# Side matmul steps as row slices, 64-bit shifts on GpSimd, and residual slots by position, in an attention block with a parallel GELU layer

## The chip, the core and the metric

The kernel runs on one NeuronCore of a Trainium2 chip. The metric is device time in microseconds of one execution. The engines are TensorE (PE in the profile, its weight loads PEld), VectorE (DVE), ScalarE (ACT), GpSimd (POOL) and the queue that issues transfers (SP).

## What is computed

A transformer block with attention and a feed-forward layer side by side, both fed by one layer norm:

```python
# x: 2048 x 512 bf16; H = 32 heads of Dh = 16; one key and one value head for all (wk, wv: 512 x 16)
xn = layernorm(x)
q = (xn @ wq) as 32 heads; k = xn @ wk; v = xn @ wv
p = softmax(q k^T * Dh**-0.5)            # 32 x 2048 x 2048
a = (p @ v, heads joined) @ wo
h = gelu_tanh(xn @ w1 + b1)              # F = 1792
out = x + a + (h @ w2 + b2)
```

## The kernel before

**Tiles and units.** The 2048 query rows are taken in four blocks of 512 (`TBW`), the heads in groups of four, so there are 32 groups (three blocks of eight, and a last block cut by quarters of its queries). A group has 64 score tiles of 128 keys x 512 columns. Three tiles in a row make a unit; there are 683 units. A unit's scores (`scores`, line 987) are three matmuls of 32 contraction rows each, one per head. They lie in three of the four 32-row groups of the array side by side, and write three PSUM banks; two halves of three banks alternate between units, so the scores of unit u+2 wait until unit u's banks are read. Unit u leaves row group (3u+3) mod 4 empty.

**Two ways to the exponential.** `DTAB` says for each tile of each unit which engine makes it. A tile not named goes to ScalarE: one ACTIVATE (`exp`, line 1026) covers the unit's one, two or three such tiles. A named tile goes to VectorE (`p1`, line 1057): it writes a 16-bit integer that, read as bf16, is a piecewise-linear power of two, and four copies shifted by constants (`SPL_STEPS`) are summed with fitted weights by TensorE. So a ScalarE tile costs TensorE one product with V, and a VectorE tile five (`pv_mm`, line 1069). Tiles of VectorE are closed into batches of one to six (`close_batch`, line 1075). A batch has three steps: the first writes one shifted copy (tile 1 from 0, +26), the second two copies (+51), both on VectorE at line 1104; the third shifts tile 0 in place (-26), one instruction per tile, written for GpSimd at line 1100, which the planner may give to VectorE.

**Side work.** Between the scores TensorE also makes the projections: q (`q_pack`, line 1195), the hidden layer (`h_mm`, 1230), and the output tiles (`out_tile`, 1302: 14 steps of `w2`, four of `wo`, one of `b2`). Each step is a 128-row contraction cut into four matmuls of 32 output columns (`mm4`, line 686). They lie in the four column groups side by side and accumulate in PSUM bank 7 (`pM`). One job at a time holds that bank; VectorE reads it out. Products with V are column-group matmuls too. So TensorE changes between row mode (a score visit) and column mode all along.

**Order.** Nothing is scheduled at run time. `Prog.schedule` (line 241) simulates the five engines with a cost for each operation and fixes each engine's order; `emit` writes it with semaphore waits. TensorE's next operation is chosen by `pick_pe`. Operations of kind `pl` (the third steps, and the normalization of the attention output, lines 1139 and 1179) are put on GpSimd under a VectorE operation that doesn't use the port that the two share; operations marked `lock` do use it. Where VectorE would be free, it takes a `pl` operation itself. The tables `HP`, `YP`, `QK`, `Q3` say at which unit each side job is released. Where TensorE would stand still for long, the planner puts in filler matmuls on zeros (line 1430).

**Residual.** An output tile needs x again: `x_load` brings it into slot 14 or 15 of `x_sb` (tile number mod 2), `out_tile` adds PSUM to it there, and `store` sends it out.

Of the kernel before, what the change touches and what calls it, by code (L numbers as in the profile page):

```python
# [5 lines left out]
dt = mybir.dt  # L6
# [34 lines left out]
PL_OCC = 0.62  # L41
# [8 lines left out]
PL_FREE = 0.06  # L50
NE_ND_KB = (23, 19, 11, 6)
# [8 lines left out]
TBL = 1  # L60
QSP = 1
# [3 lines left out]
DTAB = "o0t02o.02to.0to2o0.o.t22o.002.o0.o220t.2o.22o000.o.002ot00.o202.o200.0202.t.2t2.2t2t.20o2o0t..0.00o.o0t0o2ot0..t22tt20o202o2.ot.t.t2t.t0toto.00to.2oot.2oo002t.0t.202o.oo.22t.2o22t20.axXXo2toto.tt0t2t2.2oo202.t0tt.t0t0.oo2000o.to.0ot0.2o2t02o22t22.t220t0.20.o02.0t.0to0t22.t0..020t2o2.2.t2o2.220o02..0o00o02t...22t0oo.20t20tt.02o0t202..o2o..022to2o..02ot.00o2tt.00o0o200oo2..2t2to02o..0t0o2t2o.0tt2.2t20o..2t0ttttoo.00ot.22o.t.to222o20t.22o020..oto.o0t200ot0.0oo0.o02..22o222t..02o02ot0.0t0.2tt2.0o0t0to.0tt0000Ba0XXaot022o02.o00..too2o2.tt2o.20to00ot..2o22o0oott0o.002.o2.2tt.2t0oo0t0.ot00o.tt20.ot0.0t2.oo.0t0tt2t.2tttt.00o0tot.t2t0.0o2oo..ot22o20t200ot..t00.0t.to02o2ot0.0to2.2.t.."  # L65
YF = 664
# [48 lines left out]
class _Op:  # L115
    __slots__ = ("eng", "fn", "deps", "sdeps", "stream", "amt", "need", "ticket", "waits", "clock", "occ", "lat",
                 "allow", "kind", "tag", "nun", "outs", "rel", "lock", "pm", "rdy", "start", "end", "vis", "idx", "done", "due", "real", "docc")


class Prog:  # L120
# [19 lines left out]
    def add(self, eng, fn, r=(), w=(), acc=None, dma=None, occ=0.1, lat=0.15, allow=1.0, kind=None, tag=None, after=(), due=None, lock=False, docc=0.0):  # L140
        op = _Op()
        op.lock, op.docc = lock, docc
# [10 lines left out]
        op.pm = any(k == ("bank", 7) or k[0] == ("bank", 7) for k in w)  # L153
# [21 lines left out]
        if acc is not None:  # L175
            dep(self.writer.get(acc), False)
            for o in self.readers.get(acc, ()):
                dep(o, False)
        op.deps = list(deps.values())
# [8 lines left out]
        if acc is not None:  # L188
            self.accs.setdefault(acc, []).append(op)
# [15 lines left out]
    def pick_pe(self, t, cand, allr, mode, visit, cgbusy):  # L205
        S = [o for o in cand if o.kind == "S"]
        rest = [o for o in cand if o.kind != "S"]
# [27 lines left out]
    def rank(self):  # L235
        s0 = next(o.idx for o in self.ops if o.kind == "S")
        due = iter(PRO_DUE)
        for op in self.ops[:s0]:
            op.due = (op.due or 0.0) if op.stream != op.eng else next(due)

    def schedule(self):
# [36 lines left out]
        s_seen = False  # L278
        vleft = sum(op.kind == "v" for op in ops)
# [3 lines left out]
        def seen(o):  # L283
            return max(o.rdy + (PL_TAKE if o.kind == "pl" else 0.0), lockend) if o.lock else o.rdy

        while left:
# [12 lines left out]
            cand = [o for o in able[e] if seen(o) <= t + 1e-9]  # L299
# [100 lines left out]
            if e == "pe":  # L400
# [25 lines left out]
                elif op.kind != "side":  # L426
                    m = {"S": "row", "side": "col"}.get(op.kind, "full")
                    w = 0.0 if m == mode else SW_ROW if m == "row" else SW_COL if m == "col" else SWITCH
                    st = max([t, pend + w] + [c + w for c in cgbusy])
                    op.start = st  # L430
                    op.end = st + op.occ * slow
                    op.vis = op.end + op.lat
                    area += op.occ * (0.75 if op.kind == "S" else 1.0)
                    recent.append((st, op.occ * (0.75 if op.kind == "S" else 1.0)))
                    if m == "col":
                        cgbusy = [op.end] * 4
                    mode = m
# [11 lines left out]
            if e == "act" and op.kind in ("exp", "gelu"):  # L449
                aend = max(op.end + A_LAG, aend + op.occ + A_INC)  # L450
                op.vis = aend + A_SEM
            free[e] = max(free[e], op.end)
# [5 lines left out]
            order.append(op)  # L458
            left -= 1
            for o, cross in op.outs:  # L460
                o.nun -= 1
                v = op.vis if cross else op.end
                if v > o.rdy:
                    o.rdy = v
                if o.nun == 0:
                    ready[o.eng].append(o)
# [4 lines left out]
        for op in order:  # L471
            if op.kind == "pv":
                g, cg, first = op.tag
                op.fn = (lambda e, f=op.fn, a=first, b=last[(g, cg)] is op: f(e, a, b))
        self.nfill = nfill
# [4 lines left out]
    def settle(self):  # L480
        free = {e: 0.0 for e, _ in self.SECTIONS}
        mode, cg, pend, aend, r1 = None, [0.0] * 4, 0.0, 0.0, 0.0
        for op in self.ops:
# [3 lines left out]
            if op.eng == "pe":  # L487
                if op.kind in ("pv", "side") or (op.kind == "fill" and occ > 0.15):
# [5 lines left out]
                    mode, end = "col", t + 0.006  # L494
                else:
                    m = "row" if op.kind == "S" else "full"
# [3 lines left out]
                pend = t + (min(occ, C_OCC) if mode == "col" else occ)  # L500
            else:
# [53 lines left out]
def bass_parallel_sum__grouped_kv_mqa__dense_activation_gelu__prompt_kernel(  # L555
# [33 lines left out]
    with ExitStack() as es:  # L589
# [76 lines left out]
        def B(b):  # L666
            return ("bank", b)
# [25 lines left out]
        M4 = [(("bank", 7), j) for j in range(4)]  # L693

# [258 lines left out]
        late = [pr.writer["ibi"]]  # L953
        dma("sp", wop[:], A_wo.rearrange("(g p) n -> p g n", p=P), "d_wo", w=["wop"], after=late)
# [3 lines left out]
        dma("sp", b2row[0:1, :], B_b2.rearrange("(o n) -> o n", o=1), "d_b2", w=["b2row"])  # L958

# [27 lines left out]
        def scores(u):  # L987
# [17 lines left out]
            return add("pe", fn, r, [B(3 * x + i) for i in range(len(ts))], occ=0.216, lat=S_LAT, allow=-1.0, kind="S")  # L1005
# [68 lines left out]

        def close_batch():
# [38 lines left out]
        def o_quarter(gg):  # L1114
# [15 lines left out]
            for h in range(2):  # L1130
                for j in range(HG):
# [7 lines left out]
            o = add("pool", lambda e: e.tensor_tensor(oTq[:, 2 * k:2 * k + 2, P * q:P * q + P], v3(OfP), v3(rbP), ALU.mult),  # L1139
                    keys, [("oTq", k, q)] + (tr(8, 12) if q == 0 else []), occ=ON_OCC, lat=PL_LAT, allow=PL_DUE, kind="pl", lock=True,  # L1140
                    docc=vcost(TBW // 2))
# [5 lines left out]
        def o_evac(gg):  # L1147
# [24 lines left out]
            if h:  # L1172
# [296 lines left out]
```

## Time and profile before

| | us |
|---|---|
| median of three runs (741.23 to 741.75) | 741.59 |
| span of the profiled execution | 739.5 |
| busy: PE / DVE / ACT / POOL | 727.1 / 727.4 / 725.8 / 396.6 |

The span goes from the first to the last instruction. Busy time of an engine is time with at least one instruction open on it. Instructions on one engine overlap by their start-up, so the time from start to start is less than an instruction's mean; a matmul's 380 ns includes its way through the array, while the next four can start 0.22 us after it. The first 24 us are the layer norm and the first projections, the last 7 us the last output tile; the units fill what is between.

### The profile page before, as it was taken

What the parts mean: (1) busy time and instruction counts of PE and PEld (TensorE: products, weight loads), DVE (VectorE), ACT (ScalarE), POOL (GpSimd) and SP (SyncE); (2) the same over time, 40 slices, a digit from 0 to 9 for tenths busy, and PEclk for the clock granted to TensorE, in tenths of its full rate; (3) what the DMA queues carried; (4) which work ended last, traced back from release to release, by engine and by line L of the source; (5) the groups of instructions that cost most, each with busy time, mean ns of one, the idle gap of its engine ahead of it and who ended that gap; (6) DMA issues with size and microseconds to landing.
All of it is one profiled execution on the core that took longest, in us unless ns stands there. A gap on an engine that the chain in (4) does not pass through costs nothing.

```text
span 739.5 us, 22247 instructions
## 1 busy us (share of the span) xinstructions
PE 727.1 (98%) x9170; PEld 232.9 (31%) x9173; DVE 727.4 (98%) x1415; ACT 725.8 (98%) x760; POOL 396.6 (54%) x552
## 2 busy tenths in 40 slices
PE   7999999999999999999999999999999999999998
PEld 5333233233243332323233332232233222222323
DVE  8999999999999999999999999999999999999996
ACT  7899999999999999999999999999999999999997
POOL 8644555555524565454446545565644665555552
PEclk9999999999999999999999999999999999999999
DMA  9200100000010020101001011000100111100110
GB/s 312 67 15 17 32 10 17 24 11 19 11 42 16 13 50 17 32 14 33 24 15 35 25 32 29 22 21 11 24 17 20 29 24 32 38 22 19 24 36 26
DMA packets 36252, 23.57 MB, mean 32 GB/s; under 512 B 17768, under 2 KB 32568, under 8 KB 36152
## 3 DMA queue, kind: packets, MB, share of 16 engines
q1 hardware_dynamic: 35096, 22.12, 11.4%
q8 instruction: 73, 1.20, 0.7%
q14 instruction: 27, 0.22, 0.1%
q10 hardware_dynamic: 1056, 0.03, 0.1%
HBM read 13.28 MB, written 2.35 MB: 21 GB/s over the span
## 4 chain that ended last, share of the span: by engine, by line
ACT 68%; PE 25%; DVE 6%; DMA 1%; issue 0%; SPq 0%; POOL 0%
ACT E L1026 67%; PE pAll L1070 11%; PE pAll L1003 7%; PE pAll L689 6%; DVE Dt L1057 3%; DVE Dt L1104 2%; PE pAll L683 1%; DVE stats L780 1%; DMA x_sb<-in_A_x_dram 1%; PE pAll L836 0%; ACT xnT L841 0%; DVE ub L1234 0%; DVE Of L1151 0%; DVE Dt L1100 0%; ACT KT L854 0%
## 5 line engine op out<-in xcount | busy, mean ns | idle before, releaser
L1026 ACT ACTIVATE E<-pAll 128x1024 bf16<-128x1024 f32 (+2 forms) x678 | 675.7, 1192 | 1.4 <-PE pAll L1003 1.2
L1100 POOL TENSOR_SCALAR Dt<-Dt 128x512 int16<-128x512 int16 x456 | 351.2, 770 | 322.0 <-DVE Dt L1104 140.3
L1070 PE MATMUL pAll<-Dt,V 128*32 128x512 bf16 x2840 | 425.6, 383 | 0.9 <-DVE Of L1151 0.9
L1057 DVE TENSOR_SCALAR Dt<-pAll 128x512 int16<-128x512 f32 x555 | 379.3, 699 | 1.7 <-PE pAll L1003 0.7
L1104 DVE TENSOR_SCALAR Dt<-Dt 128x1024 int16<-128x1024 int16 (+6 forms) x542 | 296.8, 575 | 0.3
L1070 PE MATMUL pAll<-E,V 128*32 128x512 bf16 x1480 | 287.4, 385 | 0.1
L1003 PE MATMUL pAll<-QT,KT 32*128 32x512 bf16 x2048 | 267.2, 384 | 2.7 <-ACT E L1026 1.4
L1003 PEld LDWEIGHTS pAll<-QT,KT 32*128 32x128 bf16 x2048 | 66.5, 91 | 273.3 <-ACT E L1026 255.9
L1070 PEld LDWEIGHTS pAll<-Dt,V 128*32 128x32 bf16 x2840 | 113.3, 94 | 114.0 <-issue 72.0
L689 PE MATMUL pAll<-xnT,w_sb 128*32 128x512 bf16 x896 | 120.0, 382 | 0.4 <-DVE mT L1214 0.4
L1070 PEld LDWEIGHTS pAll<-E,V 128*32 128x32 bf16 x1480 | 67.2, 94 | 50.7 <-issue 37.6
L689 PE MATMUL pAll<-w_sb,ub 128*32 128x512 bf16 x448 | 71.8, 382 | 0.0
L689 PE MATMUL pAll<-w_sb,x_sb 128*32 128x512 bf16 x448 | 65.6, 382 | 0.0
L689 PEld LDWEIGHTS pAll<-xnT,w_sb 128*32 128x32 bf16 x896 | 34.8, 95 | 20.3 <-issue 9.3
L689 PE MATMUL pAll<-wop,oTp 128*32 128x512 bf16 x192 | 35.5, 384 | 0.0
L1100 DVE TENSOR_SCALAR Dt<-Dt 128x512 int16<-128x512 int16 x112 | 29.6, 291 | 0.0
L689 PE MATMUL pAll<-xnT,wq_sb 128*32 128x512 bf16 x256 | 22.2, 384 | 0.0
L1234 DVE TENSOR_SCALAR ub<-pAll,b1T 128x512 bf16<-128x512 f32 x28 | 20.9, 746 | 0.0
L689 PEld LDWEIGHTS pAll<-w_sb,x_sb 128*32 128x32 bf16 x448 | 19.2, 95 | 4.5 <-issue 1.8
L1179 POOL TENSOR_TENSOR oTp<-OfP,rbP 128x256 bf16<-128x256 f32 x24 | 18.0, 761 | 4.7 <-DVE Dt L1057 2.1
L689 PEld LDWEIGHTS pAll<-w_sb,ub 128*32 128x32 bf16 x448 | 18.2, 95 | 4.7 <-issue 2.7
L689 PE MATMUL pAll<-b2row,ones 128*32 128x512 bf16 x60 | 17.1, 381 | 0.0
(122 smaller groups left out, 275.3 us busy)
## 6 DMA issues: line engine op xcount, KB each, us to landing
w_sb<-in_B_w_dram SPq DMA_DIRECT2D x2, 1792.0 KB, 13.3
OfP<-Of SPq DMA_DIRECT2D x96, 32.0 KB, 1.9
rbP<-rden_rows SPq DMA_DIRECT2D x96, 32.0 KB, 1.8
x_sb<-in_A_x_dram SPq DMA_DIRECT2D x8, 256.0 KB, 4.6
x_sb<-in_A_x_dram SPq DMA_DIRECT2D x16, 128.0 KB, 2.2
QT<-qp SPq DMA_DIRECT2D x124, 16.0 KB, 1.8
out_dram<-x_sb SPq DMA_DIRECT2D x15, 128.0 KB, 1.8
OfP<-Of SPq DMA_DIRECT2D x56, 16.0 KB, 1.8
```

Source lines behind the costliest of these rows:

```text
L683: return add("pe", lambda e: e.matmul(o, l, rh, start=start, stop=stop, **kw), r, w, occ=occ, lat=dlat[1], allow=allow, **ak)
L689: add("pe", lambda e, c=c, j=j: e.matmul(o[c, :], l[:, c], rh, start=start, stop=stop, tile_position=(0, 32 * j)), r, [(k, j) for k in w] ...
L780: dve(lambda e, ti=ti, c=c: e.bn_stats(stats[:, c, :], x_sb[:, ti, :]), r=[("x", ti)], w=[("st", ti)], n=511)
L1003: ins = e.matmul(o, l, rh, start=True, stop=True, tile_position=(q0, 0))
L1026: o = act(lambda e: e.activation(E[:, s0:s0 + na, :], bank(b0, na).rearrange("p (a n) -> p a n", a=na), ACT.Exp, scale=LN2 / 128.0), w=[B( ...
L1057: op = dve(lambda e: e.tensor_scalar(Dt[:, s:s + n, :], bank(bk, n).rearrange("p (a n) -> p a n", a=n), float(127 * 128) + SPL_D, SPL_MIN, ...
L1070: add("pe", lambda e, a, b: e.matmul(pO[32 * j:32 * j + 32, :], V1[:, v, kt, :], rhs, start=a, stop=b, tile_position=(0, 32 * j)), r=r + [ ...
L1100: add("pool", lambda e, d=d, k=k: e.tensor_scalar(d, d, 1.0, float(k), ALU.mult, ALU.add), [], [(("D", base[o > 0] + q), o)], occ=PL_OCC, ...
L1104: dve(lambda e, d=view(o, nb), q=view(i, nb), k=k: e.tensor_scalar(d, q, float(k), None, ALU.add), r=keys(i), w=keys(o), n=nb * n * TBW, m ...
L1179: "pool", lambda e, c=c: e.tensor_tensor(oTp[0:n, sl, c], OfP[0:n, s, c], rbP[0:n, s, c], ALU.mult),
L1234: dve(lambda e: e.tensor_scalar(ubs[tb % 2][:, ft, :], pM, b1T[:, ft:ft + 1], None, ALU.add), r=["b1T"], w=M4 + [ukey(tb, ft)], n=TBW + 57 ...
```

## The change

- **Row slices.** A side step may be issued as four matmuls of 32 contraction rows and all 128 output columns (kind `rs`). Each needs one 32-row group of the array and may be issued right behind the three scores of a unit that leaves its row group empty; only one at a time may be under way, and each waits for the one before. A slice for which no visit was found 3 us after it became ready may be issued by itself. `RH`, `RQ`, `RY` give the number of steps of each job that are cut this way; the first step of a job is never one of them. Used are 22 of hidden jobs, 15 of q, and 46 of output tiles: 83 steps, 332 slices.
- **64-bit shifts.** Steps with one target (the first and the third) become `pl` operations over up to two tiles each. On GpSimd they are 64-bit adds of a constant that holds the shift four times; on VectorE they stay 16-bit. GpSimd loads another instruction library after its set-up work, and the standard one again after its last operation. The normalization of the attention output goes to VectorE, as 12 instructions of 512 columns and 7 of 256.
- **Residual slots** alternate by the order in which output tiles come.
- **Tables.** `DTAB`, the release tables and `YF` are new. By the letters of `DTAB`, VectorE makes 602 tiles (568 before), ScalarE 1446 (1480): 542 units with two ScalarE tiles (545 before), 115 with three (129), 18 with one (4), 8 with none (5). The batches are 109 of one tile, 128 of two, 36 of three, 21 of four, 8 of five or six (302 in all); before 100, 80, 64, 22, 5 (271).

```diff
-PL_OCC = 0.62
+PL_OCC = (0.398, 0.61)
+PL_N = 2
...
+RS_MAX = 3.0
+RS_GAP = 0.3
+B1U = 7
+RH = ((0,1,0,1,0,0,1,1,1,2,1,0,0,0),(3,0,1,0,0,1,1,1,1,1,1,1,1,1),(1,0,1,1,0,0,1,0,1,2,0,1,0,0),(0,0,1,0,1,1,1,1,1,1,1,1,1,1))
+RQ = ((1,1,1,1),(1,1,2,0),(0,3,0,0),(1,1,2,0))
+RY = ((3,2,3,3),(6,3,3,2),(3,4,2,4),(4,1,3,5))
...
+INT64_LIB = library_config.all_libraries[1]
+LIB_OCC = 7.0
...
 def pick_pe(self, t, cand, allr, mode, visit, cgbusy):
+        op = self.pick_main(t, cand, allr, mode, visit, cgbusy)
+        if op is None:
+            late = [o for o in cand if o.kind == "rs" and o.rdy + RS_MAX <= t + 1e-9]
+            if late and min([o.rdy for o in allr if o.kind == "S"] + [t + 9.0]) >= t + RS_GAP:
+                return min(late, key=self.due)
+        return op
...
+            if op.kind == "S" and s_seen and (rider is None or rider.vis <= op.start):
+                rs = [o for o in ready["pe"] if o.kind == "rs" and o.tag == op.tag and o.rdy <= t + 1e-9]
+                if rs:
+                    o = min(rs, key=self.due)
+                    ready["pe"].remove(o)
+                    o.start, o.end, o.vis = op.start, op.end, op.end + o.lat
...
+                    ride.append(o)
+                    if rider is not None:
+                        o.deps.append(rider)
+                        rider.need = True
+                    rider = o
...
+        def chunk(n, rows, l, rh, r, allow, js=range(4)):
+            njob[0] += n == 0
+            for j in js:
+                c = slice(32 * j, 32 * j + 32)
+                kw = dict(occ=0.216, lat=dlat[1], allow=allow, job=njob[0])
+                if 0 < n <= rows:
+                    add("pe", lambda e, b, c=c, j=j: e.matmul(pM, l[c, :], rh[c, :], start=False, stop=b, skip_group_check=True,
+                                                              tile_position=(32 * j, 0)),
+                        r, kind="rs", tag=j, accs=M4, **kw)
+                else:
+                    add("pe", lambda e, b, c=c, j=j: e.matmul(pM[c, :], l[:, c], rh, start=n == 0, stop=b, skip_group_check=True,
+                                                              tile_position=(0, 32 * j)),
+                        r, M4[j:j + 1] if n == 0 else (), kind="side", tag=(None, j), chain=M4[j] if n else None, **kw)
...
+        lib = add("pool", lambda e: e.load_library(INT64_LIB), occ=LIB_OCC, lat=0.0, after=stock, due=0.0, kind="lib")
...
-            return add("pe", fn, r, [B(3 * x + i) for i in range(len(ts))], occ=0.216, lat=S_LAT, allow=-1.0, kind="S")
+            return add("pe", fn, r, [B(3 * x + i) for i in range(len(ts))], occ=0.216, lat=S_LAT, allow=-1.0, kind="S",
+                       tag=(3 * u + 3) % HG)
...
+        def shift(e, d, x, k):
+            if e.engine == mybir.EngineType.Pool:
+                return e.int64_add(d.bitcast(dt.uint64), x.bitcast(dt.uint64), k * 0x0001000100010001 % 2 ** 64)
+            return e.tensor_scalar(d, x, float(k), None, ALU.add)
...
-                if o == i:
-                    for q in range(n):
-                        d = Dt[:, slot(o) + q, :]
-                        add("pool", lambda e, d=d, k=k: e.tensor_scalar(d, d, 1.0, float(k), ALU.mult, ALU.add),
-                            [], [(("D", base[o > 0] + q), o)], occ=PL_OCC, lat=PL_LAT, allow=PL_DUE, kind="pl", lock=True,
-                            docc=vcost(TBW, 4))
+                if nb == 1:
+                    for q in range(0, n, PL_N):
+                        w = min(PL_N, n - q)
...
+                        add("pool", lambda e, d=d, x=x, k=k: shift(e, d, x, k), kx if o != i else [], kd,
+                            occ=PL_OCC[w - 1], lat=PL_LAT, allow=PL_DUE, kind="pl", lock=True, docc=vcost(w * TBW, 4), after=[lib])
...
-            o = add("pool", lambda e: e.tensor_tensor(oTq[:, 2 * k:2 * k + 2, P * q:P * q + P], v3(OfP), v3(rbP), ALU.mult),
+            o = dve(lambda e: e.tensor_tensor(oTq[:, 2 * k:2 * k + 2, P * q:P * q + P], v3(OfP), v3(rbP), ALU.mult),
...
-                for q in range(2):
-                    c = slice(q * TBW // 2, (q + 1) * TBW // 2)
-                    onorm[gg - h] = onorm[gg] = add(
-                        "pool", lambda e, c=c: e.tensor_tensor(oTp[0:n, sl, c], OfP[0:n, s, c], rbP[0:n, s, c], ALU.mult),
...
+                onorm[gg - h] = onorm[gg] = dve(
+                    lambda e: e.tensor_tensor(oTp[0:n, sl, :], OfP[0:n, s, :], rbP[0:n, s, :], ALU.mult),
...
-            for d in range(DT):
-                mm4(pM, w1_sb[:, d, ft * P:(ft + 1) * P], xnT[:, d, tb * TBW:(tb + 1) * TBW], d == 0, d == DT - 1,
-                   r=["w1"] + tr(4 * tb, 4 * tb + 4), w=[B(7)], allow=H_ALLOW if tb < NTB - 1 else 1.5)
+            for d in range(DT):
+                chunk(d, RH[tb][ft], w1_sb[:, d, ft * P:(ft + 1) * P], xnT[:, d, tb * TBW:(tb + 1) * TBW],
+                      ["w1"] + tr(4 * tb, 4 * tb + 4), H_ALLOW if tb < NTB - 1 else 1.5)
...
+        XSL = {k: n % 2 for n, (_, k) in enumerate(sorted((YP[tb][i], (tb, i)) for tb in range(NTB) for i in range(4)))}
...
-            xr, key = x_sb[:, 14 + i % 2, :], ("x", 14 + i % 2)
+            xr, key = x_sb[:, 14 + XSL[tb, i], :], ("x", 14 + XSL[tb, i])
...
+        add("pool", lambda e: e.load_library(library_config.standard), occ=LIB_OCC, lat=0.0, after=[o for o in pr.ops if o.eng == "pool"], due=0.0, kind="lib")
```

## Rows read from the trace of the kernel before

**Rows 1.** Page: span and busy time of each engine.
```profile
span 739.5 us, 22247 instructions
PE 727.1 (98%) x9170; PEld 232.9 (31%) x9173; DVE 727.4 (98%) x1415; ACT 725.8 (98%) x760; POOL 396.6 (54%) x552
```
**Rows 2.** Waits: who waited for whom, us in total, times, longest.
```profile
PEld pAll L1003 <- ACT E L1026: 255.9, 629, 0.8
...
ACT E L1026 <- PE pAll L1003: 1.2, 3, 0.5
...
DVE Dt L1057 <- PE pAll L1003: 0.7, 2, 0.4
```
**Rows 3.** Groups by form: line, engine, shapes, count | busy, mean ns | idle.
```profile
L1026 ACT ACTIVATE E<-pAll 128x1024 bf16<-128x1024 f32 x546 | 524.4, 1114 | 0.9 <-PE pAll L1003 0.7
...
L1026 ACT ACTIVATE E<-pAll 128x1536 bf16<-128x1536 f32 x128 | 194.1, 1538 | 0.5 <-PE pAll L1003 0.5
...
L1026 ACT ACTIVATE E<-pAll 128x512 bf16<-128x512 f32 x4 | 2.6, 662 | 0.0
```
**Rows 4.** Timeline of PE in mid-run: start us, us, line, tiles, count.
```profile
304.16 0.39 PE L1003 MATMUL pAll<-QT,KT 32*128 32x512 bf16 x3
304.49 0.40 PE L1070 MATMUL pAll<-Dt,V 128*32 128x512 bf16 x3
...
304.71 0.38 PE L1070 MATMUL pAll<-E,V 128*32 128x512 bf16 x1
...
305.03 0.39 PE L1003 MATMUL pAll<-QT,KT 32*128 32x512 bf16 x3
...
305.91 0.39 PE L1003 MATMUL pAll<-QT,KT 32*128 32x512 bf16 x3
```
**Rows 5.** Groups by form: the filler matmuls.
```profile
L1430 PE MATMUL pAll<-xnT,zeros 128*32 128x512 bf16 x108 | 11.1, 389 | 0.0
```
**Rows 6.** Groups by form on DVE and POOL: p1, steps, normalization.
```profile
L1057 DVE TENSOR_SCALAR Dt<-pAll 128x512 int16<-128x512 f32 x546 | 366.4, 687 | 1.7 <-PE pAll L1003 0.7
L1100 POOL TENSOR_SCALAR Dt<-Dt 128x512 int16<-128x512 int16 x456 | 351.2, 770 | 322.0 <-DVE Dt L1104 140.3 <-PE pAll L1070 62.4 <-DVE Dt L1057 38.1
...
L1104 DVE TENSOR_SCALAR Dt<-Dt 128x1024 int16<-128x1024 int16 x180 | 74.8, 426 | 0.1
...
L1104 DVE TENSOR_SCALAR Dt<-Dt 128x2048 int16<-128x2048 int16 x102 | 69.8, 687 | 0.1
...
L1100 DVE TENSOR_SCALAR Dt<-Dt 128x512 int16<-128x512 int16 x112 | 29.6, 291 | 0.0
L1104 DVE TENSOR_SCALAR Dt<-Dt 128x512 int16<-128x512 int16 x100 | 28.1, 287 | 0.0
...
L1057 DVE TENSOR_SCALAR Dt<-pAll 128x1024 int16<-128x1024 f32 x5 | 6.0, 1222 | 0.0
...
L1139 DVE TENSOR_TENSOR xnT<-OfP,rbP 128x256 bf16<-128x256 f32 x1 | 0.4, 409 | 0.0
```
**Rows 7.** Timeline of DVE: a step of two tiles and p1 back to back.
```profile
258.04 0.69 DVE L1104 TENSOR_SCALAR Dt<-Dt 128x2048 int16<-128x2048 int16 x1
258.64 1.29 DVE L1057 TENSOR_SCALAR Dt<-pAll 128x512 int16<-128x512 f32 x2
259.84 0.35 DVE L1162 RECIPROCAL den<-den 128x32 f32<-128x32 f32 x1
```
**Rows 8.** Timeline of POOL: its first shift and some of its last ones.
```profile
27.79 0.62 POOL L1100 TENSOR_SCALAR Dt<-Dt 128x512 int16<-128x512 int16 x1
...
719.93 1.20 POOL L1100 TENSOR_SCALAR Dt<-Dt 128x512 int16<-128x512 int16 x1 [0.37 <-PE pAll L1070]
...
730.19 0.62 POOL L1100 TENSOR_SCALAR Dt<-Dt 128x512 int16<-128x512 int16 x1 [3.56 <-DVE Dt L1100]
```
**Rows 9.** Reloads: ACT's tables (by form), and a large transfer (page, DMA issues).
```profile
L1256 ACT ACT_TABLE_LOAD x2 | 2.6, 1283 | 0.0
...
w_sb<-in_B_w_dram SPq DMA_DIRECT2D x2, 1792.0 KB, 13.3
```

More of the change, by code (lines that the diff above doesn't have):

```diff
@@ L3 @@
 import concourse.bass as bass
-from concourse import mybir
+from concourse import library_config, mybir
 dt = mybir.dt
@@ L152, in add @@
         op.rel = None
-        op.pm = any(k == ("bank", 7) or k[0] == ("bank", 7) for k in w)
+        op.pm = any(k == ("bank", 7) or k[0] == ("bank", 7) for k in (*w, *accs, chain or ("",)))
         deps, sdeps = {}, {}
@@ L187, in add @@
             self.readers.setdefault(k, []).append(op)
-        if acc is not None:
-            self.accs.setdefault(acc, []).append(op)
+        for k in (*((acc,) if acc is not None else ()), *accs):
+            self.accs.setdefault(k, []).append(op)
         for o in after:
@@ L238, in rank @@
         for op in self.ops[:s0]:
-            op.due = (op.due or 0.0) if op.stream != op.eng else next(due)
+            op.due = (op.due or 0.0) if op.stream != op.eng or op.kind == "lib" else next(due)
     def schedule(self):
@@ L298, in schedule @@
             e, t = best_e, best_t
-            cand = [o for o in able[e] if seen(o) <= t + 1e-9]
+            cand = [o for o in able[e] if (o.rdy if e == "pe" else seen(o)) <= t + 1e-9]
             if e == "pe":
@@ L457, in schedule @@
             op.done = True
[L458 to L466, printed above, removed]
+            for q in [op] + ride:
+                order.append(q)
+                left -= 1
+                for o, cross in q.outs:
+                    o.nun -= 1
+                    v = q.vis if cross else q.end
+                    if v > o.rdy:
+                        o.rdy = v
+                    if o.nun == 0:
+                        ready[o.eng].append(o)
         last = {}
@@ L474, in schedule @@
                 op.fn = (lambda e, f=op.fn, a=first, b=last[(g, cg)] is op: f(e, a, b))
+        last = {}
+        for op in order:
+            if op.kind in ("side", "rs") and op.job:
+                for j in range(4) if op.kind == "rs" else (op.tag[1],):
+                    last[op.job, j] = op
+        final = {id(o) for o in last.values()}
+        for op in order:
+            if op.kind in ("side", "rs") and op.job:
+                op.fn = (lambda e, f=op.fn, b=id(op) in final: f(e, b))
         self.nfill = nfill
@@ L494, in settle @@
                     mode, end = "col", t + 0.006
+                elif op.kind == "rs" and mode == "row" and prev in ("S", "rs"):
+                    t, end = pend - occ, pend
                 else:
-                    m = "row" if op.kind == "S" else "full"
+                    m = "row" if op.kind in ("S", "rs") else "full"
                     w = 0.0 if m == mode else SW_ROW if m == "row" else SWITCH
@@ L1273, in gelu, with y_mm, wo_mm @@
             gelu_after[u + 1] = o
-        def y_mm(tb, i, start=True, stop=False, bk=7, fts=range(FT), al=1.5):
-            for ft in fts:
-                mm4(bank(bk), ubs[tb % 2][:, ft, i * P:(i + 1) * P], w2_sb[:, ft, :], start and ft == fts[0], stop and ft == fts[-1],
-                   r=[ukey(tb, ft), "w2"], w=[B(bk)], allow=al)
-        def wo_mm(tb, i, ps, start=False, bk=7, al=1.5, stop=False):
+        def y_mm(tb, i, al, rows=None):
+            for ft in range(FT):
+                l, rh, r = ubs[tb % 2][:, ft, i * P:(i + 1) * P], w2_sb[:, ft, :], [ukey(tb, ft), "w2"]
+                if rows is None:
+                    mm4(pM, l, rh, ft == 0, False, r=r, w=[B(7)], allow=al)
+                else:
+                    chunk(ft, rows, l, rh, r, al)
+        def wo_mm(tb, i, ps, al, rows=None):
             for n, p in enumerate(ps):
```

90 lines of the change are left out of this document (56 added, 34 removed).

## The prediction

> **What bounds the kernel now.** I read the page's busy shares first, then the waits, then the groups by form, and last the timeline of single engines. The shares name no bottleneck: PE, DVE and ACT are each busy 98% of the span, and only POOL has room, at 54% [rows 1]. The waits say that this is no accident of counting. ACT waited for TensorE's scores 1.2 us in all, and DVE's p1 0.7 us [rows 2]. The largest entry, the scores' weight loads behind ACT for 255.9 us in 629 waits, looks like a TensorE with room to spare, but it is the loader that waits. The timeline of PE shows why [rows 4]: a score visit at 304.16, the first four columns 0.33 us later, the next four 0.22 us after them, the next score visit 0.32 us after that. The unit before 305.91 has the same 0.87 us rhythm. The 0.33 and 0.32 us are the changes between row and column mode, so the array doesn't stand still either. The 678 exponentials have 1.4 us of idle time among them [rows 3], and on DVE a step and two p1 follow one another without a gap [rows 7].
>
> So three engines are full at once, and relieving one alone gives nothing. The change must be added up on each, and the smallest relief is the gain.
>
> **ScalarE.** By the letters of the tables, 34 tiles go from ACT to DVE. An ACTIVATE of three tiles takes 1538 ns and one of two 1114 ns, so a tile is 0.424 us [rows 3]: 34 x 0.424 = 14.4 us. There are three instructions fewer (675 for 678); at 662 - 424 = 0.24 us each that would be 0.7 us more, but their start-up overlaps. I take 14.6 us off.
>
> **TensorE.** Removed from the column visits: 83 steps of four matmuls, each step 0.22 us as in rows 4: 18.3 us. Added: each of the 34 tiles needs five products with V where it needed one, 136 matmuls, 34 rounds of four, 7.5 us. The 332 slices ride behind scores. No row shows a fourth row group. From below a slice costs nothing, since the score visit is there anyway and a gain has no source; from above it costs a whole round, 0.22 us, as if it queued. The nearest row is the score visit itself: three matmuls are through in 0.39 us where one takes 384 ns, so each further one costs some 0.003 us [rows 3, 4]. I take 0.005 us, 1.7 us in all. Each slice also waits for the slice before it, on TensorE's own queue, and the whole unit is queued behind that; but the earlier slice went with an earlier unit, at least 0.87 us before, and takes about 0.4 us, so the wait is over. Net: 18.3 - 7.5 - 1.7 = 9.1 us. To this comes what TensorE wastes now: 108 fillers, 27 rounds [rows 5], 27 x 0.22 = 5.9 us in which it had nothing else to do. So between 9.1 and 15.0 us can be had.
>
> **VectorE.** Means there contain 0.09 us of overlap: p1 has a mean of 0.69 us [rows 6] and goes from start to start in 0.60 [rows 7]. With it taken off, a step of one, two or four tiles takes 0.20, 0.34 and 0.60 us [rows 6], which is 0.07 + 0.13 for each tile.
> - First steps leave: 271 x 0.07 + 568 x 0.13 = 92.8 us. Third steps that DVE did itself: 112 x 0.20 = 22.4 us.
> - Second steps grow by 31 batches and 34 tiles of two targets: 31 x 0.07 + 68 x 0.13 = 11.0 us. p1 grows by 13 or 14 instructions and 34 tiles at 1222 - 687 = 0.53 us [rows 6]: 18.9 us.
> - The normalization comes: 12 of 512 columns, between a p1's 0.60 and twice the 256-column one's 0.32 (409 ns less overlap), and six more of 256: 7.2 + 1.9 = 9.1 us. They wait for their transfers on DVE's queue with p1 behind them, which POOL didn't have to mind; at most the 0.4 us of rows 2 each, 7.6 us. I take nothing, since the planner sets them after the landing.
>
> Net 76.2 us off. Against it stand the shifts that DVE takes back. There are 227 two-tile and 148 one-tile shifts for each of the two steps, 750 in all, at 0.34 and 0.20 us on DVE. If DVE is to be only as much shorter as ACT, it may take 61 us of them, some 215, and POOL has to do about 535.
>
> **GpSimd.** No row shows a 64-bit add. From above: today's instruction, 0.62 us for one tile when undisturbed [rows 8], so 0.62 and 1.24; from below a quarter of the elements, 0.16 and 0.31. I take the diff's own 0.398 and 0.61, because the planner's figures for what the trace does show are right: 0.62 for today's shift against 0.62 in rows 8, 0.216 for a matmul against 0.22. Then 535 x 0.53 = 282 us, where POOL spends 351 us on shifts alone now [rows 6], and a two-tile add fits under one p1 as today's shift does. The Trainium skill's page "SBUF — State Buffer" (the table of doors) gives GpSimd 4 bytes per lane and cycle at 1.2 GHz; a tile is 1,024 bytes in a partition, an estimate of 0.21 us for each tile, the very difference of the two figures. No run so far shows it.
>
> **Library.** No row shows a load. The nearest are ACT's table load, 1.28 us, and a 1.8 MB transfer, 13.3 us [rows 9]. The diff plans 7.0 us, and I take that, as no row speaks for another value. At the head, POOL's first shift comes at 27.79 us [rows 8]; for 7 us more DVE does the shifts, at 0.20 us for each of about six, 1 us of DVE. At the end, POOL's last shift is over at 730.81, 8.7 us ahead of the end [rows 1, 8], so a reload of 7 us is covered and one of 13.3 costs 4.6 us. The residual slots cost nothing: x comes long ahead and the adding is the same.
>
> **The sum.** ACT -14.6, DVE free to follow, TensorE -9.1 to -15.0. I take ACT's, less 1.0 us for places where TensorE can't use the filler time: 739.5 - 13.6 = 725.9 us of span. The median is 2.1 us above the span (741.59 against 739.5), so **728.0 us**.
>
> **Rivals.**
> 1. *TensorE becomes the bound.* The fillers stand where nothing was ready, and slices make jobs hold bank 7 longer: a step needs four visits with four different row groups, about four units. Then only 9.1 us less some riders that cost 0.01 us, about 7.5 us: 739.5 - 7.5 + 2.1 = 734 us. For it: the 0.87 us rhythm without a gap [rows 4]. Against: the fillers. Chance 0.18.
> 2. *The 64-bit add is longer than planned, and the kernel is slower.* Place: POOL's adds under p1. A two-tile add planned at 0.61 us just lasts as long as a p1; what is longer runs into VectorE's next step, and the two can't use the port together: a shift that met a VectorE step took 1.20 instead of 0.62 us [rows 8]. The same page of the Trainium skill calls the port pair an exclusive lock, held for the whole instruction by whoever starts first; the row agrees for one side. Of 535 adds some 320 are of two tiles. At today's mean of 0.77 us (0.16 over plan) and with half of them ahead of a step: 160 x 0.16 = 26 us of DVE, so 728 + 26 = 754 us. It decides from 13.6 / 160 = 0.085 us over plan, at 0.70 us. For it: POOL's mean is 0.15 above its own undisturbed time now [rows 6, 8]. Against: the planner's other figures hold. Chance 0.13.
> 3. *A slice doesn't ride, it queues.* 332 x 0.22 = 73 us against 18.3 saved: about 785 us; it decides at 13.6 / 332 = 0.04 us each. Against: three row groups run side by side [rows 4]. Chance 0.04.
> 4. *The library takes longer.* At 13.3 us, 6.3 us are lost at the head and 4.6 at the end: 739 us; halfway 733. The Trainium skill's "GPSIMD Engine Reference" (Instruction dispatch) has about 6 us for the first call after a load. By that, both loads are covered. Chance 0.05.
>
> **The numbers.** Forecast 0.60, rivals 0.18, 0.13, 0.04, 0.05. A measurement of this kernel tells about 0.2% from no change, 1.5 us. Faster: the forecast, rival 1 and most of rival 4, 0.80; the same 0.04; slower 0.16. The range goes down to 720, where the 5.9 us of fillers are gained besides as better filled units, and up to 742, with rivals 1 and 4 and the first part of rival 2: some 0.8.
>
> **What would show it.** Right: ACT still without idle time, with 675 exponentials; score visits with a fourth matmul and the same 0.32 us to the columns; no third or first step on DVE but for some 215; POOL's adds near 0.40 and 0.61 us. Wrong: waits of ACT for scores well above 1.2 us (rival 1); steps on DVE that start late behind POOL, and products with V that wait for POOL (rival 2); the columns 0.2 us later behind a slice (rival 3); POOL empty far past 34 us, or its reload as the last thing of the span (rival 4).

## The result and the profile after

The changed kernel takes 729.99 us (729.94 to 730.21), in the same session as 741.67 us for the kernel before: a ratio of 0.9842, 95% interval 0.9828 to 0.9856. That is 11.7 us off. The forecast was 728.0 us, with a range from 720 to 742. The profiled execution has a span of 728.2 us, 11.3 us less than before [rows 1].

Page of the changed kernel, span and busy time of each engine:

```profile
span 728.2 us, 22534 instructions
PE 713.9 (98%) x9301; PEld 223.5 (31%) x9301; DVE 691.4 (95%) x1243; ACT 712.8 (98%) x757; POOL 418.2 (57%) x669
```

ACT's busy time fell by 13.0 us and PE's by 13.2, against a span that fell by 11.3. DVE fell by 36.0 us. So DVE now has room (busy 95% of the span, 98% before), while ACT and PE are as full as they were. Groups by form of the changed kernel (line, engine, shapes, count | busy us, mean ns | idle before), to be held against rows 3, 5 and 6:

```profile
L1104 ACT ACTIVATE E<-pAll 128x1024 bf16<-128x1024 f32 x543 | 515.0, 1094 | 1.2 <-PE pAll L761 0.3 <-PE pAll L1080 0.2
L1155 POOL INT64_ADD Dt<-Dt x603 | 396.2, 666 | 289.9 <-DVE Dt L1135 116.2 <-DVE Dt L1188 70.1 <-DVE Dt L1156 42.0
L1135 DVE TENSOR_SCALAR Dt<-pAll 128x512 int16<-128x512 f32 x544 | 360.3, 681 | 19.3 <-PE pAll L761 14.0 <-PE pAll L1080 4.2
...
L1104 ACT ACTIVATE E<-pAll 128x1536 bf16<-128x1536 f32 x114 | 169.0, 1515 | 0.9 <-PE pAll L1080 0.5
...
L1156 DVE TENSOR_SCALAR Dt<-Dt 128x1024 int16<-128x1024 int16 x66 | 26.4, 414 | 0.0
...
L1156 DVE TENSOR_SCALAR Dt<-Dt 128x512 int16<-128x512 int16 x81 | 22.2, 281 | 0.0
...
L1104 ACT ACTIVATE E<-pAll 128x512 bf16<-128x512 f32 x18 | 11.9, 661 | 0.0
...
L1515 PE MATMUL pAll<-xnT,zeros 128*32 128x512 bf16 x100 | 10.2, 387 | 0.0
...
L1260 DVE TENSOR_TENSOR oTp<-OfP,rbP 128x512 bf16<-128x512 f32 x12 | 8.2, 680 | 0.0
```

The 675 exponentials still have some 2 us of idle time. GpSimd does 603 of the 750 shifts and DVE 147 (66 + 81). p1 now has 19.3 us of idle time before it, where it had 1.7 [rows 6]. And 100 of the 108 fillers are still there.

A slice in the timeline of PE (start us, us, line, tiles, count):

```profile
684.38 0.39 PE L1080 MATMUL pAll<-QT,KT 32*128 32x512 bf16 x3
684.38 0.39 PE L761 MATMUL pAll<-w_sb,x_sb 32*128 32x512 bf16 x1
684.70 0.40 PE L1148 MATMUL pAll<-E,V 128*32 128x512 bf16 x3
...
685.68 0.39 PE L1080 MATMUL pAll<-QT,KT 32*128 32x512 bf16 x3
685.69 0.39 PE L761 MATMUL pAll<-w_sb,x_sb 32*128 32x512 bf16 x1
686.00 0.40 PE L1148 MATMUL pAll<-E,V 128*32 128x512 bf16 x3
```

The slice (L761) starts with the three scores and is through with them. The columns come 0.32 us after the scores, as they came 0.33 us after them without a slice [rows 4]. Over the whole trace 326 of the 332 slices ride on a score visit and six are issued by themselves. From the first score of a visit to its first column matmul it is 325 ns in the median with a slice (323 visits that columns follow) and 321 ns without one (349 visits): a slice costs 4 ns.

Timeline of POOL, head and tail:

```profile
26.54 0.53 POOL L1032 MEMSET b2row<- 128x512 bf16 x1
32.57 0.19 POOL L1030 MEMSET b1row<- 128x128 bf16 x1 [5.50 <-issue]
32.76 0.39 POOL L1155 INT64_ADD Dt<-Dt  x1
...
711.35 0.40 POOL L1155 INT64_ADD Dt<-Dt  x1 [0.44 <-DVE Dt L1135]
...
715.40 0.61 POOL L1155 INT64_ADD Dt<-Dt  x1 [2.17 <-DVE Dt L1188]
718.25 0.61 POOL L1155 INT64_ADD Dt<-Dt  x1 [2.24 <-DVE Dt L1188]
```

The 5.50 us gap with nothing to wait for is the library's load. Undisturbed, the adds take 0.40 us for one tile and 0.61 us for two. Their mean is longer, 0.67 us over all 603 (L1155 above), where these two values would give 0.54: on average an add stands open 0.13 us longer than it takes undisturbed. The last one ends at 718.86, 9.3 us ahead of the end.

Where DVE has room is seen in stretches (busy us and instructions of each engine, then clock, DMA share, GB/s):

```profile
204.00:354.00 150.00, 149.03 (x2043) 46.27 (x2038) 142.05 (x246) 148.79 (x148) 78.87 (x126) 1.00 0.10 26
...
684.00:721.00 37.00, 36.91 (x531) 12.03 (x523) 26.34 (x49) 36.72 (x35) 9.24 (x16) 1.00 0.14 37
```

The columns are PE, PEld, DVE, ACT and POOL. In the last stretch DVE is busy for 26.34 of 37 us. The two last groups of heads have 12 and 13 tiles on DVE, where most others have 16 to 20.

### The profile page after: what moved, and what is told of

Its sections match the earlier page's. It is cut to its first block, busy times and chain, and to the rows that moved or that the text cites. A ratio compares the mean times of both kernels' runs of the same rounds, so it can differ in the third digit from the quotient of the medians.

```text
span 728.2 us, 22534 instructions
## 1 busy us (share of the span) xinstructions
PE 713.9 (98%) x9301; PEld 223.5 (31%) x9301; DVE 691.4 (95%) x1243; ACT 712.8 (98%) x757; POOL 418.2 (57%) x669
## 4 chain that ended last, share of the span: by engine, by line
ACT 55%; PE 37%; DVE 7%; DMA 1%; issue 0%; POOL 0%; SPq 0%
ACT E L1104 55%; PE pAll L1148 18%; PE pAll L1080 11%; PE pAll L765 4%; DVE Dt L1135 3%; PE pAll L747 2%; DVE Dt L1188 2%; PE pAll L741 1%; DVE stats L854 1%; DMA x_sb<-in_A_x_dram 1%; PE pAll L910 0%; PE pAll L761 0%; DVE x_sb L1314 0%; DVE qp L1280 0%; DVE Dt L1156 0%
## 5 line engine op out<-in xcount | busy, mean ns | idle before, releaser
L1155 POOL INT64_ADD Dt<-Dt x603 | 396.2, 666 | 289.9 <-DVE Dt L1135 116.2
L1135 DVE TENSOR_SCALAR Dt<-pAll 128x512 int16<-128x512 f32 (+2 forms) x570 | 394.1, 711 | 21.5 <-PE pAll L761 16.1
L1188 DVE TENSOR_SCALAR Dt<-Dt 128x1024 int16<-128x1024 int16 (+4 forms) x302 | 202.4, 680 | 1.4 <-PE pAll L1148 0.7
L1156 DVE TENSOR_SCALAR Dt<-Dt 128x1024 int16<-128x1024 int16 (+1 forms) x147 | 46.9, 341 | 0.1
L765 PE MATMUL pAll<-w_sb,x_sb 128*32 128x512 bf16 x304 | 46.5, 382 | 0.0
L765 PE MATMUL pAll<-w_sb,ub 128*32 128x512 bf16 x352 | 45.4, 382 | 0.0
L761 PE MATMUL pAll<-w_sb,ub 32*128 32x512 bf16 x96 | 36.9, 385 | 0.0
L761 PE MATMUL pAll<-w_sb,x_sb 32*128 32x512 bf16 x88 | 33.8, 384 | 0.1
L761 PE MATMUL pAll<-xnT,w_sb 32*128 32x512 bf16 x88 | 33.8, 384 | 0.1
L765 PEld LDWEIGHTS pAll<-xnT,w_sb 128*32 128x32 bf16 x520 | 20.3, 94 | 10.6 <-issue 6.8
L761 PE MATMUL pAll<-xnT,wq_sb 32*128 32x512 bf16 x60 | 23.1, 384 | 0.0
```

What stands on the lines that cost most here:

```text
L761: add("pe", lambda e, b, c=c, j=j: e.matmul(pM, l[c, :], rh[c, :], start=False, stop=b, skip_group_check=True, tile_position=(32 * j, 0)), ...
L765: add("pe", lambda e, b, c=c, j=j: e.matmul(pM[c, :], l[:, c], rh, start=n == 0, stop=b, skip_group_check=True, tile_position=(0, 32 * j)) ...
L1135: op = dve(lambda e: e.tensor_scalar(Dt[:, s:s + n, :], bank(bk, n).rearrange("p (a n) -> p a n", a=n), float(127 * 128) + SPL_D, SPL_MIN, ...
L1155: return e.int64_add(d.bitcast(dt.uint64), x.bitcast(dt.uint64), k * 0x0001000100010001 % 2 ** 64)
L1156: return e.tensor_scalar(d, x, float(k), None, ALU.add)
L1188: dve(lambda e, d=view(o, nb), q=view(i, nb), k=k: e.tensor_scalar(d, q, float(k), None, ALU.add), r=keys(i), w=keys(o), n=nb * n * TBW, m ...
```

## The experiments

All of them keep the order of instructions that the planner made for their kernel, so that what they show isn't a new plan. All but the last change prices in it; the last changes an address. Where they leave out columns, the kernel leaves out that part of its result.

**Is one engine the bound before the change?** Four kernels relieve one engine, or several, by about the change's own 14 us.

```diff
 b_act:
-  e.activation(E[:, s0:s0 + na, :], bank(b0, na)..., ACT.Exp, ...)
+  e.activation(E[:, s0:s0 + na, 0:500], bank(b0, na)...[:, :, 0:500], ACT.Exp, ...)
 b_dve:
-  e.tensor_scalar(Dt[:, s:s + n, :], bank(bk, n)..., ...)
+  e.tensor_scalar(Dt[:, s:s + n, 0:488], bank(bk, n)...[:, :, 0:488], ...)
 b_pe (the steps of RH, RQ, RY):
-  e.matmul(o[c, :], l[:, c], rh, ...)
+  e.matmul(o[c, 0:32], l[:, c], rh[:, 0:32], ...)
```

(In `b_act` and `b_dve` the first use of each buffer is whole, so that nothing unwritten is read. The fourth kernel, `b_all`, has all three edits.)

> The kernel before in its own order, but the 83 side steps that the change turns into slices write 32 of their 512 columns (the rest of these products is left out), so TensorE is relieved of 83 x (0.22 - 0.03) = about 16 us and nothing else changes. Theory (three engines are full at once, so relief of one gives nothing): 739 to 742 us. Rival A (TensorE alone sets the pace): 725 to 729 us. Rival B (ScalarE alone sets it): 741 us.

> The kernel before in its own order, but every exponential on ScalarE covers 500 of each tile's 512 columns (the other 12 keep old values), so ScalarE is relieved of 1480 x 12 / 1.2 GHz = about 14.5 us and nothing else changes. Theory (three engines full at once): 739 to 742 us. Rival A (TensorE alone): 741 us. Rival B (ScalarE alone): 727 to 729 us.

> The kernel before in its own order, but every p1 on VectorE covers 488 of each tile's 512 columns, so VectorE is relieved of 568 x 0.025 = about 14 us and nothing else changes. Theory (three engines full at once): 739 to 742 us. Rivals A and B: 741 us. If VectorE alone sets the pace: 727 to 729 us.

> All three reliefs together in the order of the kernel before (83 side steps with 32 of 512 columns, exponentials with 500, p1 with 488). Theory (three engines full at once): 726 to 731 us, as the change itself. Rival A: as with TensorE's relief alone. Rival B: as with ScalarE's relief alone.

| kernel | us | ratio to before, 95% interval |
|---|---|---|
| b_pe | 741.18 | 0.9995 (0.9985 to 1.0005) |
| b_act | 739.28 | 0.9965 (0.9952 to 0.9978) |
| b_dve | 740.97 | 0.9991 (0.9981 to 1.0000) |
| b_all | 733.61 | 0.9896 (0.9881 to 0.9910) |

Before was 741.60 us. The single reliefs give 0.4, 2.3 and 0.6 us, 3.3 in sum. Together they give 8.0. That is the sign of engines that are full at once, though the 726 to 731 expected of the three together were missed by 2.6 us. One reason is seen in the trace: b_pe hardly relieves TensorE, so it didn't test what it was made for, and b_all has the same edit. PE's busy time fell from 727.1 to 725.9 us. Timeline of PE in b_pe:

```profile
268.62 0.39 PE L1007 MATMUL pAll<-QT,KT 32*128 32x512 bf16 x3
268.94 0.40 PE L1074 MATMUL pAll<-E,V 128*32 128x512 bf16 x3
268.95 0.35 PE L693 MATMUL pAll<-w_sb,ub 128*32 128x32 bf16 x2
269.17 0.38 PE L1074 MATMUL pAll<-Dt,V 128*32 128x512 bf16 x2
...
269.49 0.39 PE L1007 MATMUL pAll<-QT,KT 32*128 32x512 bf16 x3
```

The cut matmuls (128x32) run beside whole ones of other column groups. Those start 0.23 us after the round before all the same, and the visit is 0.87 us long as in rows 4. So a second kernel shortened every column matmul but the first of its sum.

```diff
-  e.matmul(pO[32 * j:32 * j + 32, :], V1[:, v, kt, :], rhs, ...)
+  e.matmul(pO[32 * j:32 * j + 32, 0:492], V1[:, v, kt, :], rhs[:, 0:492], ...)     # and the same in mm4
```

> The kernel before in its own order, with every column-group matmul but the first of its sum on 492 of 512 columns (the last 20 columns of those products are left out), so that each round of four on TensorE is 20 / 2.4 GHz = 8 ns shorter: about 1870 rounds, 15 us of relief for TensorE alone. The earlier run with 83 steps cut didn't relieve it, since a cut matmul shares its round with whole ones. Theory (three engines are full at once): 0 to 4 us off, 737 to 741 us. Rival A (TensorE alone sets the pace, before and after): 726 to 730 us.

741.04 us against 741.50, ratio 0.9994 (0.9984 to 1.0004). Timeline of PE in it:

```profile
304.05 0.39 PE L1004 MATMUL pAll<-QT,KT 32*128 32x512 bf16 x3
304.37 0.39 PE L1071 MATMUL pAll<-Dt,V 128*32 128x492 bf16 x3
...
304.59 0.37 PE L1071 MATMUL pAll<-E,V 128*32 128x492 bf16 x1
...
304.97 0.39 PE L1004 MATMUL pAll<-QT,KT 32*128 32x512 bf16 x3
```

The matmuls are shorter, but the next scores start 0.38 us after the second round, where it was 0.32 [rows 4], and the visit takes 0.92 us. TensorE was relieved and stood waiting. The whole traces say the same. A measure of the wait is the time from the start of a visit's last column matmul to the next scores, as far as it is above its median (some 670 to 680 changes a kernel; a_act is told of below):

| kernel | median, ns | mean, ns | above the median in sum, us |
|---|---|---|---|
| before | 312 | 319 | 4.5 |
| b_pe492 | 304 | 326 | 15.1 |
| b_act | 312 | 314 | 1.5 |
| after | 312 | 319 | 4.7 |
| a_act | 312 | 316 | 2.9 |

With shorter rounds TensorE waits 10.6 us more. With shorter exponentials the wait falls by 3.0 us, near the 2.3 us that b_act won: there wasn't more to win on ScalarE alone.

So before the change neither TensorE, nor ScalarE, nor VectorE set the pace alone: this is shown by the three single reliefs. That the gain comes when they are relieved together is shown by b_all as far as it goes. Two things were not run: a pair of reliefs, so it isn't shown that VectorE had to be among them, and all three in full at once, apart from the change itself.

**What a slice costs.**

```diff
-  e.matmul(pM, l[c, :], rh[c, :], start=False, ...)
+  e.matmul(pM[:, 0:32], l[c, :], rh[c, 0:32], start=False, ...)
```

> The changed kernel in its own order, with every one of the 332 row slices cut to 32 of its 512 columns (the rest of those products is left out), so that whatever a slice costs beside the scores goes. Theory (a slice rides at some 0.005 us): 728 to 730 us, at most 1.7 us off. Rival 3 (a slice queues for its own 0.2 us): 665 to 690 us. Half way (0.04 us each, the point at which the slices would have eaten the gain): about 717 us.

730.84 us, ratio to before 0.9847 (0.9830 to 0.9863), where the changed kernel has 0.9842. Taking 94% of the slices' columns away gives nothing. That alone would leave a price that doesn't depend on the columns, but the 325 against 321 ns above rule it out: 326 x 0.004 = 1.3 us. The slices ride. What they are worth isn't shown by a run: none turned them back into column steps in the changed kernel, so how much of the 11.7 us is theirs, and how much is the new tables', is argued from the counts of rounds only.

**What a longer add would cost.**

```diff
-  e.int64_add(d.bitcast(dt.uint64), x.bitcast(dt.uint64), k * 0x0001000100010001 % 2 ** 64)
+  e.tensor_scalar(d, x, 1.0, float(k), ALU.mult, ALU.add)      # and no library
```

> The changed kernel in its own order, with GpSimd's 603 shifts written as 16-bit adds of the same one or two tiles, and no library loaded. The price goes from 0.40 and 0.61 us to some 0.62 and 1.2 us. Theory (rival 2 of the prediction as a mechanism: an add that outlasts the p1 it lies under meets VectorE's next step, and products with V wait for it): 388 two-tile adds 0.6 us longer, half of them in the way, 116 us more, 800 to 870 us. Rival (GpSimd is busy 57%, so there is room): 730 to 750 us.

841.48 us, ratio 1.1338 (1.1321 to 1.1355): 111.5 us more than the changed kernel. Groups by form on POOL in it:

```profile
L1155 POOL TENSOR_SCALAR Dt<-Dt 128x1024 int16<-128x1024 int16 x388 | 456.9, 1177 | 108.6 <-DVE Dt L1188 31.0 <-DVE Dt L1135 23.0 <-DVE Dt L1156 15.3
L1155 POOL TENSOR_SCALAR Dt<-Dt 128x512 int16<-128x512 int16 x215 | 167.3, 778 | 69.7 <-DVE Dt L1135 16.7 <-DVE Dt L1156 11.7 <-DVE Dt L1188 11.1
```

And its waits (who waited for whom: us in total, times, longest):

```profile
PEld pAll L1148 <- POOL Dt L1155: 91.0, 173, 1.6
...
PE pAll L1148 <- POOL Dt L1155: 27.6, 59, 1.3
```

GpSimd is busy 77% of that span, so it isn't full; it is late. The 388 two-tile adds have a mean of 1.18 us, where the same adds in the changed kernel have 0.74, and the 215 one-tile adds 0.78 for 0.54 (the order is the same, so the sizes can be matched one by one). In sum they are 388 x 0.44 + 215 x 0.24 = 222 us longer, and products with V wait for them; VectorE's own busy time is 84.8 us longer (776.2 for 691.4) with the same instructions. The loss of 111.5 us is half of the 222. The expectation's 116 us came from half as well, but its working took the two-tile adds as 0.6 us longer, which is too much, and left the one-tile adds out; the two errors nearly cancel.

**What a longer library load would cost.**

```diff
-  lib = add("pool", lambda e: e.load_library(INT64_LIB), ...)
+  lib = add("pool", lambda e: (e.load_library(INT64_LIB), e.load_library(library_config.standard), e.load_library(INT64_LIB))[-1], ...)
```

> The changed kernel with two more library loads behind one another at the head (64-bit, standard, 64-bit), all else the same: GpSimd is empty until about 44 instead of 33 us. The trace shows 5.5 us for one load. Theory (a load longer than planned is lost one for one, as nothing before the first shifts is idle): 11 us more, 739 to 742 us. Rival (the order has slack at the head and takes it back): under 3 us more, 730 to 733 us.

744.41 us, ratio 1.0032 (1.0021 to 1.0043): 14.4 us more than the changed kernel, more even than expected. Timeline of POOL in it:

```profile
26.92 0.52 POOL L1032 MEMSET b2row<- 128x512 bf16 x1
46.50 0.19 POOL L1030 MEMSET b1row<- 128x128 bf16 x1 [19.06 <-issue]
46.70 1.74 POOL L1155 INT64_ADD Dt<-Dt  x3
```

The gap is 19.06 us for three loads, 13.6 us more than for one. It is lost, and 0.8 us besides. But GpSimd's lateness need not be all of the 14.4 us. The first matmul behind the gap in the timeline of PE:

```profile
47.14 0.61 PE L1148 MATMUL pAll<-Dt,V 128*32 128x512 bf16 x2 [11.37 <-POOL Dt L1155]
```

And stretches of the same trace (busy us and instructions of PE, PEld, DVE, ACT and POOL, then the granted TensorE clock, DMA share, GB/s):

```profile
36.00:42.00 6.00, 0.00 (x0) 0.00 (x0) 0.00 (x0) 0.82 (x1) 0.00 (x0) 0.86 0.00 0
42.00:48.00 6.00, 0.61 (x2) 0.10 (x2) 0.88 (x2) 0.00 (x0) 1.50 (x4) 0.50 0.00 1
48.00:54.00 6.00, 5.98 (x37) 1.18 (x37) 4.25 (x9) 3.80 (x3) 2.38 (x3) 0.50 0.07 17
54.00:60.00 6.00, 6.00 (x80) 1.80 (x77) 5.82 (x14) 5.67 (x7) 2.65 (x3) 1.00 0.04 10
```

TensorE stands still for 11.4 us, waiting for GpSimd, and then runs on at a granted clock of 0.50, 1.2 GHz, until 54 us, where the changed kernel has 1.00 from 24 to 60 us. So "one for one" isn't cleanly shown: how the 14.4 us divide between the load and the clock stays open. What is shown is that the order has no slack at the head to take them back.

**What bounds the kernel after the change.** The same reliefs on the changed kernel; TensorE's is the cut of the last four `w2` steps of 15 output tiles.

```diff
 a_act: as b_act.   a_pe (a_peact has both):
-  chunk(ft, rows, l, rh, r, al)
+  chunk(ft, rows, l, rh, r, al, cut=ft >= 10)      # 32 of 512 columns
```

> The changed kernel in its own order, with the exponentials on ScalarE on 500 of 512 columns: 1446 x 12 / 1.2 GHz = 14.5 us of relief for ScalarE alone. Theory (TensorE and ScalarE share the bound after the change): 1 to 4 us off, 726 to 729 us. Rival A (TensorE alone is the bound now): 730 us. Rival B (ScalarE alone, as the forecast's sum took it): 715 to 718 us.

> The changed kernel in its own order, with the last four w2 steps of 15 output tiles (60 steps, 240 column matmuls) cut to 32 of 512 columns: TensorE alone is relieved of 60 x (0.22 - 0.03) = about 11 us. Theory (TensorE and ScalarE share the bound after the change): 1 to 4 us off, 726 to 729 us. Rival A (TensorE alone is the bound now): 718 to 720 us.

> The changed kernel in its own order, with both reliefs: TensorE by about 11 us (60 side steps cut) and ScalarE by about 14.5 us (exponentials on 500 of 512 columns). VectorE, which has 95% busy time after the change, is left as it is. Theory (TensorE and ScalarE share the bound, VectorE has room): more than the two alone together, 6 to 10 us off, 720 to 724 us. Rival (VectorE is a third bound still, as before the change): hardly more than each alone, 726 to 729 us.

| kernel | us | ratio to before, 95% interval |
|---|---|---|
| after | 729.99 | 0.9842 (0.9828 to 0.9856) |
| a_act | 728.83 | 0.9821 (0.9807 to 0.9836) |
| a_pe | 730.34 | 0.9849 (0.9833 to 0.9865) |
| a_peact | 727.45 | 0.9811 (0.9796 to 0.9825) |

a_act is 1.2 us faster than the changed kernel, though the intervals overlap. a_pe is no faster, where 726 to 729 was expected. a_peact is 2.5 us faster, outside the intervals, which is the rival's number and not the theory's. ScalarE alone is not the bound: it gives back 1.2 of 14.5 us. Of TensorE this shows little, since a_pe has the fault of b_pe. Pages of a_pe and a_act, busy time:

```profile
PE 713.0 (98%) x9301; PEld 224.9 (31%) x9301; DVE 691.7 (95%) x1243; ACT 712.9 (98%) x757; POOL 417.4 (57%) x669
PE 713.0 (98%) x9301; PEld 223.6 (31%) x9301; DVE 690.3 (95%) x1243; ACT 707.6 (97%) x757; POOL 417.8 (57%) x669
```

In a_pe, PE's busy time fell from 713.9 to 713.0 us only. The table of waits above adds one thing: in the changed kernel the scores wait 4.7 us in all, so a faster ScalarE alone can win back little more than that. TensorE's other waits, inside its column visits, aren't in that table. Whether TensorE would be faster if it were relieved in earnest, or would then wait for ScalarE, or for VectorE in the stretches in which that is still full, stays open; a kernel with shorter rounds, as b_pe492, wasn't run on the changed one.

**The residual slots.**

```diff
-  XSL = {k: n % 2 for n, (_, k) in enumerate(sorted(...))}
+  XSL = {(tb, i): i % 2 for tb in range(NTB) for i in range(4)}
```

> The changed kernel with one part undone: the residual's slot is the tile number mod 2 again instead of its place in the order of tiles. Theory (x comes long before it is added): 729 to 731 us, no difference. Rival (two neighbours in the order would share a slot and the second load would wait for the first tile's store): 732 us or more.

729.93 us, ratio 0.9846 (0.9831 to 0.9860): no difference. With the slots by number, tiles 1 and 3 of the first block, now neighbours in the order, share a slot, and the planner's program order puts the second load ahead of the first addition, so that some rows get another tile's x. The part is needed by the new tables and costs no time.

## Why the prediction was right

**Three full engines.** This was the reading on which the sum rested, and the single reliefs bear out that none of the three set the pace alone: 0.5, 2.3 and 0.6 us for some 14 us on PE, ACT and DVE.

**The smallest relief.** The forecast took ScalarE's relief as the smallest and the gain, less 1.0 us. The runs don't bear out that choice. If ScalarE set the pace of the changed kernel, a_act would have taken 715 to 718 us; it took 728.83. The small wait of the scores speaks for rival 1's mechanism, a full TensorE, with more relief than the 7.5 us that it gave; but that isn't shown, as no run relieved TensorE in the changed kernel by more than a trifle. That 13.6 us forecast and 11.3 us measured lie so near is in part luck: ScalarE's sum, 14.6, and TensorE's bounds, 9.1 to 15.0, lay in the same place.

**ScalarE, -14.6 forecast.** 675 exponentials stand in the trace, as counted. ACT's busy time fell by 13.0 us, 1.6 less than the sum; what that is wasn't separated. Its idle time in the span rose from 739.5 - 725.8 = 13.7 to 728.2 - 712.8 = 15.4 us. 13.0 - 1.7 = 11.3.

**TensorE, -9.1 to -15.0 forecast.** PE's busy time fell by 13.2 us, inside the bounds. The slice's price, 0.005 us, is 0.004 in the trace. It was taken from this group of the kernel before, which no row shows:

```profile
L1003 PE MATMUL pAll<-QT,KT 32*128 32x512 bf16 x2048 | 267.2, 384 | 2.7 <-ACT E L1026 1.4 <-ACT KT L854 0.2 <-DVE Of L1151 0.2
```

The term that was mis-sized is the fillers: the sum gave 5.9 us for them, and 13.6 us needed 4.5 of these on top of the 9.1. 100 of 108 are still there, 8 x 0.22 / 4 = 0.4 us. So the places where TensorE has nothing to do have stayed. But 9.1 + 0.4 is 9.5, and the span fell by 11.3, so the sum has other errors too. Counted in both traces from the first score to the last, the column visits (to the next scores) take 486.7 us before and 469.6 after, 17.1 less, where the sum's 18.3 - 7.5 + 0.4 is 11.2. The score visits (to the next columns) take 220.5 and 226.2 us, 5.7 more, of which the riding slices are 1.3 and the sum had 1.7. Why the columns gave more and the visits took more wasn't separated; the two errors offset each other for the most part. Rival 1, which gave up the fillers altogether and let a slice cost 0.01 us, came to 734 us: 4.0 us too much, where the forecast was 2.0 too little.

**VectorE.** Forecast was that DVE would take back some 215 shifts and come out even with ACT. It took 147, and has 36.0 us less to do. The sum itself held: 76.2 us off before the shifts, and 66 x 0.33 + 81 x 0.20 = 38 us of shifts on DVE, leave 38 us off, against the 36.0 measured. What failed is the assumption that the three engines would come out even: TensorE and ScalarE got less relief than VectorE, and 18.6 us of its 36.8 us of idle time lie in the two stretches shown above. The normalization at 680 ns (0.60 from start to start) is the lower of the two bounds, as taken. The 7.6 us allowed for its waits didn't come up.

**GpSimd.** The one price that no row could show was right for an undisturbed add: 0.40 and 0.61 us for the diff's 0.398 and 0.61. The reason given, that the planner's other figures agree with the trace, was a good one here. The Trainium skill's "SBUF — State Buffer" (the table of doors) has 4 bytes per lane and cycle at 1.2 GHz for GpSimd, an estimate of 0.21 us for 1,024 more bytes a partition; the trace agrees, with 0.21 us between the two sizes. What POOL would spend was put too low: 282 us forecast, 396.2 measured, since it does 603 adds and not 535, and their mean is 0.67 us and not 0.53. Rival 2 was the right danger: with today's instruction in the same order the kernel is 111.5 us slower. But its sign was the wrong one. By it a two-tile add over 0.70 us was to eat up the gain; the mean here is 0.74 us, and the gain stands. A mean with waiting in it was not the price to compare with the plan here.

**Library.** 5.5 us at the head, less than the 7.0 planned. The Trainium skill's "GPSIMD Engine Reference" (Instruction dispatch) has about 6 us for the first call after a load; the trace's gap of 5.5 agrees nearly. The reload at the end has 9.3 us of cover; at 5.5 us it would be over 3.8 us ahead of the end. It has no line of its own in the trace. Rival 4's price was right in kind: a longer load at the head is lost, 14.4 us for 13.6, with part of it perhaps the clock's.

## What to carry to other kernels

When several engines are full at once, add a change up on each of them, and take the smallest relief, not the sum; a single relief of 14 us was worth 0.5 to 2.3 us here. Then ask of the changed kernel once more which engine is the bound: here it wasn't ScalarE alone, whose relief the forecast took. A matmul that needs only some rows of the array could ride beside others for 4 ns here. Shortening some matmuls of a round of column groups, while whole ones stay in it, gave nothing that could be measured. And in an order fixed beforehand an engine with 40% of its time free is no cover: where its instructions outgrew the slots that were planned for them, half of the growth came back as lost time.

## What the runs showed of the hardware

- A matmul in a fourth row group beside three scores costs 4 ns (325 for 321 ns to the columns); cutting all 332 slices to 32 columns won nothing (730.84 us, 729.99 with whole ones).
- Cutting some column-group matmuls from 512 to 32 columns didn't bring forward the whole ones beside them: in b_pe those still started 0.23 us after the round before.
- An undisturbed 64-bit add on GpSimd takes 0.40 us for 128 and 0.61 us for 256 elements a partition; a 16-bit add of the same bytes takes 0.62 and 1.04 us undisturbed (a_shift16). With the waiting in them the means are 0.54 and 0.74 us against 0.78 and 1.18.
- One library load on GpSimd left a gap of 5.5 us, three in a row 19.06 us.
- With TensorE standing still from 35.8 to 47.1 us of the span (a_lib3), its granted clock was 0.86 in the mean of the stretch from 36 to 42 us, 0.50 (1.2 GHz) from 42 to 54 us, and 1.00 (2.4 GHz) again in the stretch from 54 to 60 us.
